# Two of twenty stores cut by partitions: 96 rows in one transfer, 32 rows in four transfers of eight

## The chip, the cores and the metric

The kernel runs on one core of a Trainium2 chip. The metric is the device time of one execution in microseconds (us); less is better. A core has a tensor engine (PE, with its weight loads listed as PEld), a vector engine (DVE), a scalar engine (ACT), GpSimd (POOL) and a sync engine (SP). Transfers between the chip's memory (HBM) and the on-chip buffer (SBUF, 128 partitions) are issued by ACT, SP and POOL and carried out by 16 DMA engines. Products of PE land in PSUM banks and are copied out by DVE or ACT.

## The reference

Inputs are `q`, `k`, `v` of 4 x 6400 x 256 in float32, a temperature `tau` of 1, gate weights (256 x 8), and adapter weights `A` (8 x 256 x 16) and `B` (8 x 16 x 256). The output is 25600 x 256 in float32.

```python
qn = q / (np.linalg.norm(q, axis=1, keepdims=True) + 1e-06)
kn = k / (np.linalg.norm(k, axis=1, keepdims=True) + 1e-06)
s = kn.transpose(0, 2, 1) @ qn / tau            # 256 x 256 for each batch
a = softmax of s over the last axis
x = (v @ a).reshape(25600, 256)

logits = x @ w_gate                             # 8 experts
topk = the two largest of each row;  w = softmax of those two
delta[row] = sum over the two experts e of  w * (x[row] @ A[e]) @ B[e]
return x + delta
```

So each batch needs all of its `q` and `k` before any row of its output can be made: the 256 x 256 matrix `a` is a sum over all 6400 rows. After that, rows of `v` are independent of each other.

## The kernel before

**Tiling.** A batch's 6400 rows lie in SBUF as 128 partitions of 50 chunks: partition p has the 50 consecutive rows from 50 p on. Two chunks are a pair, 25 pairs to a batch, 100 in all. Five pairs are a group: its result tile `ys` is 128 partitions x 10 chunks x 256 floats, so the part of a partition is 10,240 bytes, consecutive in HBM too. There are 20 such groups; the last one is cut into groups of three and two pairs.

**Loads.** POOL issues nearly all loads (lines 148, 149 and 151), and they turn float32 into bf16 on the way. `load_more` issues the next one as soon as its buffer is free: four buffers for slices of `q` and `k`, three for pieces of `v`. SP issues the first chunks of `q` and `k` and the weights.

**Two interleaved streams.** The first batch's Gram matrix (`gram`, line 217) and norms (`square`, `norm`) run alone. Then a loop over slots handles a pair of output work per slot, while the Gram matrices of batches 1, 2 and 3 are worked off beside it, in the slots 0 to 20, 24 to 45 and 49 to 67. For a pair, `transposes` brings `v` onto the other axis (line 366) and copies it to `vT` (line 375 on ACT, 377 on DVE); `logits` and `gating` make the gate of a group; `z_gz`, `gz_t` and `delta` make the adapters' part; `y_mm` (line 488) multiplies by `a`. `delta` adds the adapters' part in the same PSUM bank (line 508), and ACT copies the bank to `ys` (line 512). There are two banks for `y` and two for the transposes.

**Stores.** When a group's last pair has been copied, the group goes onto the list `unsent`. `send` (line 522), called once a slot, issues a store from ACT's queue (line 529) while the list is longer than `keep`. `keep` is 7 until slot 67 and falls by one every four slots after it, so that the stores wait while the loads run, and the first goes out at 145.9 us. The pool of `ys` tiles has nine buffers: the first copy of a group waits until the store of the group nine before it has landed. The last ten pairs are stored in seven smaller transfers from SP's queue (line 516). Store number i of ACT's queue, counted from 0, is group i; its 18 stores are groups 0 to 17.

The order of each engine's instructions is written out by the program. On a queue they are issued in that order, and an instruction that waits on a semaphore holds up all behind it on the same engine. Each transfer raises a semaphore as it lands; the transfers of ACT and SP take eight semaphores in turn.

The change touches `send`, and with it lines 522 to 529.

Of the kernel before, what the change touches and what calls it, by code (L numbers as in the profile page):

```python
# [16 lines left out]
def kernel(  # L17
# [18 lines left out]
    P = 128  # L36
# [11 lines left out]
    GRP = 5  # L48
    QKB, VB, YB = 4, 3, 9
    VP = [18, 16, 16]  # L50
    FIRST = 4
    DEFER = 7

    GRAM = {1: (0, 20), 2: (24, 45), 3: (49, 67)}
    assert B == 4 and NC == 50
# [4 lines left out]
    out_v = out.rearrange("(b p c) d -> b p c d", b=B, p=P)  # L60
# [23 lines left out]
    for b, (first, last) in GRAM.items():  # L84
        n = last - first + 1
# [255 lines left out]
    for b in range(B):  # L341
        f = 0
# [179 lines left out]
    def send(keep):  # L522


        eng = nc.scalar
        while len(unsent) > keep:
            gr = unsent.pop(0)
            c0, n = 2 * (gr["f"] - gr["b"] * NPAIR), 2 * gr["n"]
            eng.dma_start(out_v[gr["b"], :, c0:c0 + n, :], gr["ys"][:, 0:n, :])


    for c in range(0, NC, 2):
# [40 lines left out]
    while nz < NPT or zq is not None or dq is not None:  # L573
# [4 lines left out]
        f, us, fb = (None, 0.0, 0) if behind else at_chain.get(slot, (None, 0.0, 0))  # L578
# [19 lines left out]
        if dq is not None:  # L598
            delta(dq)
        dq, zq = zq, u  # L600
        send(max(0, min(DEFER, DEFER - (slot - GRAM[B - 1][1]) // 4)))
        if behind:
            deal(0.3)
# [52 lines left out]
```

## Time and profile before

| | us |
|---|---|
| Median of three runs | 255.92 (255.84 to 256.08) |
| Profiled execution, timed | 255.87 |
| Its span, first to last instruction | 254.1 |
| Busy: PE / ACT / DVE / POOL | 220.4 / 176.1 / 152.7 / 33.0 |
| ACT's stores: first and last issue | 145.9 / 235.8 |
| ACT's stores: issue to landing, least / median / most | 11.0 / 13.1 / 16.1 |
| SP's last store: issue | 246.12 |
| TensorE's mean granted clock | 0.966 of full speed |

The span is counted from the core's first instruction, and all times of the trace are in us from there. In the page, a row of digits cuts the span into 40 slices and gives the busy share of each in tenths. A line of the stretches' view gives start and end, its length, then for PE, PEld, DVE, ACT and POOL the busy time and the number of instructions, then the granted clock, the mean busy share of the 16 DMA engines, and the GB/s that they moved. A line of the waits' view gives who waited for whom, the sum in us, how many times, and the longest. A row of the queues gives packets, MB, and the time of the packets as a share of 16 engines' span; q0 is POOL's queue, q10 ACT's, q1 SP's, and q8 and q14 carry instructions. The trace also holds every packet's start and duration (without the number of its engine), and every landing: a semaphore of a transfer is raised 16 times.

### The profile page before, as it was taken

The numbers are of one execution on the slowest core, as the hardware profiler recorded it, in microseconds if no ns is written. First come the engines' busy times: TensorE is split into PE (matmuls) and PEld (weight loads), VectorE is DVE, ScalarE is ACT, GpSimd is POOL, SyncE is SP. The second block draws the span as 40 slices with busy tenths as digits, with TensorE's granted clock in tenths as the row PEclk, the third lists the DMA queues.
The fourth block names the chain that finished last, engine by engine and source line by source line (L and its number), as shares of the span: only waits on it lengthen the run. The fifth ranks groups of instructions, "written<-read, shape, count | busy, mean of one in ns | idle before, by whom it ended". The sixth has DMA issues, their size and how long they took to land.

```text
span 254.1 us, 7393 instructions
## 1 busy us (share of the span) xinstructions
PE 220.4 (87%) x3106; PEld 190.2 (75%) x3106; DVE 152.7 (60%) x577; ACT 176.1 (69%) x290; POOL 33.0 (13%) x67
## 2 busy tenths in 40 slices
PE   0787793985999999999999989999999899999950
PEld 0444461775899978989999778989997799998940
DVE  1322235453567678685776876767587876778720
ACT  3434344776488698887878778888867777887860
POOL 8131221112112100110110202000000200000000
PEclk9999998696899999999999999999999999999997
DMA  7999999999999999999999999999999999999995
GB/s 213 223 217 215 212 216 214 213 216 216 210 214 215 223 207 215 218 212 214 215 220 211 214 270 259 236 296 281 255 291 292 389 326 362 414 420 426 423 412 220
DMA packets 13745, 66.80 MB, mean 263 GB/s; under 512 B 2576, under 2 KB 2704, under 8 KB 10384
## 3 DMA queue, kind: packets, MB, share of 16 engines
q0 software_dynamic: 8496, 38.80, 74.8%
q10 hardware_dynamic: 2592, 23.59, 22.4%
q1 hardware_dynamic: 2624, 3.94, 4.7%
q8 instruction: 24, 0.39, 0.6%
q14 instruction: 9, 0.07, 0.1%
HBM read 78.91 MB, written 26.21 MB: 414 GB/s over the span
## 4 chain that ended last, share of the span: by engine, by line
PE 58%; DMA 25%; DVE 7%; ACT 3%; issue 2%; POOL 1%; DVEq 0%; POOLq 0%; ACTq 0%
DMA qk<-in_k_dram 20%; PE y_ps L488 15%; PE acc L217 11%; PE zg L472 7%; PE y_ps L508 7%; PE vT_ps L366 6%; DMA out_dram<-ys 5%; PE zg L496 4%; PE nrm L234 3%; PE vT_ps L387 3%; ACT sq L207 2%; DVE gz L476 2%; ACT ys L512 1%; DVE lm L422 1%; DVE e L418 1%
## 5 line engine op out<-in xcount | busy, mean ns | idle before, releaser
L207 ACT ACTIVATE sq<-qk 128x1024 bf16<-128x1024 bf16 x87 | 89.6, 1054 | 22.1 <-DMA qk<-in_k_dram 16.8
L217 PE MATMUL acc<-qk 128*128 128x256 bf16 x400 | 74.7, 287 | 15.3 <-DMA qk<-in_k_dram 8.8
L512 ACT COPY ys<-y_ps 128x512 f32<-128x512 f32 x100 | 58.8, 588 | 22.9 <-PE y_ps L508 19.7
L488 PE MATMUL y_ps<-a_bf,vT 128*128 128x256 bf16 x400 | 60.3, 273 | 0.3 <-ACT ys L512 0.3
L217 PEld LDWEIGHTS <-qk 128*128 128x128 bf16 x400 | 34.4, 102 | 25.4 <-DMA qk<-in_k_dram 11.8
L476 DVE TENSOR_TENSOR gz<-zg,gate 128x256 bf16<-128x256 f32 x100 | 41.7, 418 | 14.7 <-PE zg L472 13.4
L377 DVE COPY vT<-vT_ps 128x512 bf16<-128x512 bf16 x63 | 26.7, 424 | 28.2 <-PE vT_ps L366 27.6
L234 PEld LDWEIGHTS <-sq 128*128 128x128 bf16 x600 | 36.3, 98 | 7.2 <-ACT sq L207 3.1
L366 PE MATMUL vT_ps<-ident,vt 128*128 128x128 bf16 x400 | 39.5, 223 | 0.9 <-DMA vt<-in_v_dram 0.7
L472 PE MATMUL zg<-wa_sb,vT 128*128 128x128 bf16 x400 | 38.7, 220 | 1.2 <-DVE gzT L502 1.0
L508 PE MATMUL y_ps<-ball_sb,gzT 128*128 128x256 bf16 x200 | 38.2, 273 | 0.0
L234 PE MATMUL nrm<-ones_bf,sq 128*128 128x1 bf16 x600 | 35.9, 165 | 1.2 <-ACT sq L207 1.2
L488 PEld LDWEIGHTS <-vT 128*128 128x128 bf16 x400 | 33.6, 97 | 3.2 <-issue 0.4
L366 PEld LDWEIGHTS <-vt 128*128 128x128 bf16 x400 | 30.2, 99 | 3.4 <-DMA vt<-in_v_dram 0.8
L496 PE MATMUL zg<-ident,gz 128*128 128x128 bf16 x200 | 27.9, 222 | 1.1 <-DVE gz L476 0.6
L375 ACT COPY vT<-vT_ps 128x512 bf16<-128x512 bf16 x37 | 21.7, 587 | 10.3 <-PE vT_ps L366 8.9
L472 PEld LDWEIGHTS <-vT 128*128 128x128 bf16 x400 | 26.1, 97 | 3.4 <-issue 2.2
L502 DVE COPY gzT<-zg 128x256 bf16<-128x256 bf16 x90 | 25.3, 281 | 0.0
L148 POOL DMA_DIRECT2D qk<-in_q_dram x21 | 11.4, 545 | 91.1 <-ACT sq L207 23.6
L209 DVE TENSOR_TENSOR sq<-qk 128x1024 bf16<-128x1024 bf16 x13 | 9.0, 693 | 22.3 <-DMA qk<-in_k_dram 15.4
L496 PEld LDWEIGHTS <-gz 128*128 128x128 bf16 x200 | 15.3, 99 | 2.9 <-DVE gz L476 2.5
L151 POOL DMA_DIRECT2D vt<-in_v_dram x17 | 9.0, 534 | 64.4 <-PE y_ps L508 45.5
(61 smaller groups left out, 183.6 us busy)
## 6 DMA issues: line engine op xcount, KB each, us to landing
out_dram<-ys ACTq DMA_DIRECT2D x18, 1280.0 KB, 13.1
qk<-in_q_dram POOLq DMA_DIRECT2D x18, 640.0 KB, 20.9
qk<-in_k_dram POOLq DMA_DIRECT2D x18, 640.0 KB, 23.1
vt<-in_v_dram POOLq DMA_DIRECT2D x5, 1024.0 KB, 26.9
vt<-in_v_dram POOLq DMA_DIRECT2D x3, 1152.0 KB, 25.3
vt<-in_v_dram POOLq DMA_DIRECT2D x6, 512.0 KB, 22.1
out_dram<-ys SPq DMA_DIRECT2D x3, 512.0 KB, 8.7
out_dram<-ys SPq DMA_DIRECT2D x4, 256.0 KB, 7.6
```

The costliest lines, as they stand in the source:

```text
L207: nc.scalar.activation(sq, src, ACT.Square)
L217: nc.tensor.matmul(acc[b][:, ic, :], t[:, 1, o, ic * P:(ic + 1) * P], t[:, 0, o, :], start=(c == 0 and ic == 0), stop=(c == NC - 1), skip_ ...
L234: nc.tensor.matmul(nrm[b][:, j:j + 1], sq[:, w, c % 2, ic * P:(ic + 1) * P], ones_bf[:, 0:1], start=(c == 0 and j == 0), stop=(c == NC - 1 ...
L366: nc.tensor.matmul(pt[:, ic, sc * P:(sc + 1) * P], vt[:, o + sc, ic * P:(ic + 1) * P], ident, is_transpose=True, start=(i == 0), stop=(i = ...
L377: nc.vector.tensor_copy(dst, src)
L472: nc.tensor.matmul(z[:, sc, :], r["vT"][:, ic, sc, :], st[b]["wa"][:, ic, E:E + ER], start=(sc == 0 and ic == 0), stop=(sc == 1 and ic == ...
L476: nc.vector.tensor_tensor(out=gz.rearrange("p c (e r) -> p c e r", e=E), in0=z.rearrange("p c (e r) -> p c e r", e=E), in1=gr["gate"][:, r ...
L488: nc.tensor.matmul(y[:, sc, :], r["vT"][:, ic, sc, :], st[b]["a"][:, ic, :], start=(sc == 0 and ic == 0), stop=False, skip_group_check=True)
L496: nc.tensor.matmul(gt[:, sc, :], r["gz"][:, sc, :], ident, is_transpose=True, start=(sc == 0), stop=(sc == 1))
L502: nc.vector.tensor_copy(gzT, gt)
L508: nc.tensor.matmul(r["y"][:, sc, :], r["gzT"][:, sc, :], ball_sb, start=False, stop=(sc == 1), skip_group_check=True)
L512: nc.scalar.copy(gr["ys"][:, r["w"]:r["w"] + 2, :], r["y"])
```

## The change

The stores of groups 4 and 9 are issued as five transfers each. The first has partitions 0 to 95; the other four have eight partitions each, 96 to 103 and so on up to 127. All five come from ACT's queue, one after the other, and the bytes are the same. All other stores stay one transfer of 128 partitions.

```diff
     FIRST = 4
     DEFER = 7
+    TILTED = (4, 9)
...
         while len(unsent) > keep:
             gr = unsent.pop(0)
             c0, n = 2 * (gr["f"] - gr["b"] * NPAIR), 2 * gr["n"]
-            eng.dma_start(out_v[gr["b"], :, c0:c0 + n, :], gr["ys"][:, 0:n, :])
+            ends = [0, 96, 104, 112, 120, P] if gr["f"] // GRP in TILTED else [0, P]
+            for p0, p1 in zip(ends, ends[1:]):
+                eng.dma_start(out_v[gr["b"], p0:p1, c0:c0 + n, :], gr["ys"][p0:p1, 0:n, :])
```

`gr["f"]` is the number of a group's first pair among the 100, and `GRP` is 5, so `gr["f"] // GRP` is the group's number.

## The prediction

> **What bounds the kernel now.** I read the page first: engines, DMA rows, queues.
>
> ```profile
> span 254.1 us, 7393 instructions
> PE 220.4 (87%) x3106; PEld 190.2 (75%) x3106; DVE 152.7 (60%) x577; ACT 176.1 (69%) x290; POOL 33.0 (13%) x67
> ...
> DMA  7999999999999999999999999999999999999995
> ...
> q0 software_dynamic: 8496, 38.80, 74.8%
> q10 hardware_dynamic: 2592, 23.59, 22.4%
> q1 hardware_dynamic: 2624, 3.94, 4.7%
> q8 instruction: 24, 0.39, 0.6%
> q14 instruction: 9, 0.07, 0.1%
> HBM read 78.91 MB, written 26.21 MB: 414 GB/s over the span
> ```
>
> No compute engine is full over the span; the 16 DMA engines are, in every slice but the first and last. The queues' shares add up to 103%. So each DMA engine works without a pause from the first load to the last store, and it ends when its own sum of work is done. The page cannot show whether all sixteen end together. Busy time by stretches can; the last two columns are the DMA share and GB/s.
>
> ```profile
> 230.00:245.00 15.00, 14.55 (x187) 12.99 (x185) 10.56 (x49) 12.41 (x31) 0.00 (x0) 1.00 1.00 420
> ...
> 248.00:249.00 1.00, 0.00 (x0) 0.00 (x0) 0.00 (x0) 0.00 (x0) 0.00 (x0) 1.00 1.00 393
> 249.00:249.40 0.40, 0.00 (x0) 0.00 (x0) 0.00 (x0) 0.00 (x0) 0.00 (x0) 1.00 0.86 338
> 249.40:249.80 0.40, 0.00 (x0) 0.00 (x0) 0.00 (x0) 0.00 (x0) 0.00 (x0) 1.00 0.70 282
> ...
> 250.20:250.60 0.40, 0.00 (x0) 0.00 (x0) 0.00 (x0) 0.00 (x0) 0.00 (x0) 0.62 0.61 241
> ...
> 251.40:251.80 0.40, 0.00 (x0) 0.00 (x0) 0.00 (x0) 0.00 (x0) 0.00 (x0) 0.50 0.60 230
> ...
> 252.20:252.60 0.40, 0.00 (x0) 0.00 (x0) 0.00 (x0) 0.00 (x0) 0.00 (x0) 0.50 0.34 128
> 252.60:253.00 0.40, 0.00 (x0) 0.00 (x0) 0.00 (x0) 0.00 (x0) 0.00 (x0) 0.50 0.03 10
> ```
>
> Compute ends before 247. After 249 the DMA share steps down: six engines of sixteen stop by 250.2, ten (0.60 to 0.65) go on to about 252. The last store's semaphore has sixteen landings, one for each engine's share; read from the trace's records, as us after the first at 249.36:
>
> ```
> 0.00 0.06 0.16 0.22 0.28 0.96 | 2.61 2.75 | 3.29 3.32 3.38 3.47 3.55 3.63 3.67 3.69
> ```
>
> Six are early, two in the middle, eight last; the last lands at 253.04, and the timed 255.87 of this execution is 2.83 more (the median of three, 255.92, is 0.05 above it). Where the lags come from: q8 has 24 packets with 0.6% of 16 x 254.1 us, about 1.0 us each. In the records their durations repeat with a period of eight (936, 975, 974, 961, 893, 893, 951, 945 ns, then nearly the same again, twice). I read that as eight engines in turn, three fetches each, some 3.0 us: the last eight. Of the middle two, one ran its 10,240-byte packets at about 420 ns instead of 385 through most of 187 to 246 us; the other, I think, took six of the nine q14 packets, 0.32 us each.
>
> **The change, part by part.** Two stores of 18, the fifth (issued 190.86) and the tenth (208.44), become five transfers each.
>
> Who moves the rows. q10 holds 18 x 128 packets of 10,240 bytes, so a row is a packet and each engine has eight rows of a store today. An eight-row transfer has eight packets and reaches at most eight engines. If all four begin on the same eight, those have 6 + 4 = 10 rows of the group and the others six. Two groups: plus four rows here, minus four there. Nothing in this trace has fewer than 128 rows in a store, so the bounds are: rows spread evenly (0 us), or four more on eight fixed engines, 4 x 0.385 = 1.54 us, with eight more completion packets of 9 to 22 ns (the 4-byte packets of q10), about 0.1: 1.64 us. I take the second, because a transfer of eight equal rows has no reason to begin elsewhere than the last one did. The Trainium skill, page "DMA: Bandwidth & Descriptors", section "Why a DMA increments its semaphore by 16 and not by 1", states that a transfer uses the largest number of engines up to 16 that divides its rows, and on these queues the lowest-numbered ones: 16 for 96 rows, the same eight for eight rows. No run here shows it yet.
>
> What that does to the end. Eight engines get 1.64 us more, but only six are early. At least two of the ten later ones are among the receivers. At best these are the middle two, with the receivers the eight that have no q8 fetches: the later becomes 2.75 + 1.64 = 4.39 after 249.36, against 3.69 now, so +0.70 us; the last eight fall to 3.69 - 1.54 = 2.15, which no longer matters. If one of the last eight is a receiver, the end moves by the whole 1.54 to 1.64. Even work would end near 3.69 - 1.36 = 2.33 (the shares missing from 1.00 between 249.0 and 252.6, in steps of 0.4 us, sum to 3.39 x 0.4 = 1.36 us per engine), but this tilt overshoots: 1.64 is more than the 0.94 between middle and last.
>
> What ACT pays. Issues cost ACT's sequencer this much:
>
> ```profile
> L529 ACTq DMA_DIRECT2D out_dram<-ys x18: 338/338/621, 145.9 to 235.8; - x18
> ...
> DMA to landing us min/median/max: 11.0/13.1/16.1
> ```
>
> The two long ones, 0.57 at 199.33 and 0.62 at 229.13, follow another issue closely. Four more, back to back: 4 x 0.34 = 1.4 to 4 x 0.62 = 2.5 us for each group; I take 2.3, as these follow each other. Behind them queue the copies of line 375 (vT, which frees PE's transpose bank) and line 512 (which frees y). At 190.86 the block is partly covered: ACT sits idle 1.68 us until 194.55 anyway, for the fourth store to land (the only such wait, below). At 208.44 nothing covers it but ACT's slack of about 20%, and PE, busy 9.9 of 10 us from 210, slips by 1 to 2 us. In sum 2 to 3.3 us of compute.
>
> ```profile
> ACT ys L512 <- DMA out_dram<-ys: 1.7, 1, 1.7
> ```
>
> Semaphores. ACT's and SP's transfers take eight semaphores in turn, and one whose predecessor has not landed waits on its queue. Eight more transfers are one whole turn, so the last stores keep their partners. Between, each waits for a nearer one: the thirteenth store (217.76) would need the ninth, landed at 219.23, or 218.4 if two rows fewer lie ahead on the late engines: 0 to 1.5 us on ACT, I take 0.5; PE's transposes and y wait for that. The first copies into the two groups' reused y tiles wait for five landings; their extra waits are 17 ns each.
>
> What hides it: the last SP store is issued at 246.12 and lands 6.9 us later, because the engines have older rows. From an empty queue the first load of the run landed 3.6 us after its issue, with rows twice as long; I take 3.0 for that store. So compute may slip by 3.9 us before it sets the end; 2.5 to 3.8 us fit. If the cover were gone, it would all be added. SP's own stores move with the copies; POOL's queue is issued past 200.0 no more, and its loads of 198.97 to 200.0 come up to two rows (0.8 us) later on receivers, earlier elsewhere.
>
> Against splitting at all speaks the same page, section "Rules for kernel authors": one 128-partition transfer of 1 MiB or more, no splitting by partitions, as both parts run on the same engines. Its section "Anatomy of one DMA — SWDGE (gpsimd) path" has a fixed 2.0 us per transfer for another kind of queue; eight more would be 16 us if they added up. The row here: SP's last two stores, 256 KB each, land 0.63 us apart, 416 GB/s, so a fixed part is not paid one after the other, and in the sum it is nothing.
>
> Sum: 0.70 us on the two middle engines, compute hidden. 255.92 + 0.70 = 256.6.
>
> **Rivals.**
> Receivers include some of the last eight (all, or every second engine). For it: nothing in the trace numbers the engines. Against: two sets of eight would have to cross. 255.92 + 1.54 = 257.5.
>
> No tilt: the small transfers are spread or begin in turn. For it: no 8-row store in the trace. Then only ACT's cost remains, hidden: 255.9 to 256.1.
>
> Faster: the middle two are not late in the run that is timed. The slow packets belong to one engine, come and go (385 ns again between 205 and 218), and the timed runs of before, bound by the last eight, say nothing on them. The end is then the engine at 0.96 + 1.64 = 2.60 after 249.36 against 3.69: 254.8. It decides where both middle lags are under 3.69 - 1.64 = 2.05. Against it: six q14 packets are work that comes in every execution.
>
> ACT's slip beyond its cover: at 5 us of slip, 1.1 over, 257.0. It takes PE to lose more than ACT's whole added issue time.
>
> **How the numbers follow.** Middle engines decide: 0.45 (own range 256.2 to 257.0; a quarter of it within 0.2%). Receivers among the last: 0.20. ACT's slip: 0.03. No tilt: 0.12. Faster: 0.20. A measurement tells about 0.2%, 0.5 us, from no change. Slower: 0.34 + 0.20 + 0.03 + 0.02 of no tilt = 0.59. Same: 0.10 + 0.09 + 0.02 of the faster case = 0.21. Faster: 0.18 + 0.01 + 0.01 = 0.20. The range, 255.1 to 257.7, leaves out most of the faster case (0.14) and the top of the others (0.05).
>
> **What would show it.** Five issues of line 529 at the fifth and tenth store, 0.34 to 0.62 us each. Right: the small transfers' landings come from eight engines only, the lags of the two sets shift by 1.64 + 1.54 = 3.2 us against each other, all engines but two stop by about 251.3, and the DMA share is 0.1 to 0.2 from there to about 253.4. Wrong: a share that falls from 1.00 to nothing within 1 us near 251.5 (faster), ten engines to the end as now (no tilt), or about half of them until 254.6 (receivers late). The prediction fails too if SP's last store goes out after 250.

## The result and the profile after

The changed kernel takes 258.94 us (median; 258.41 to 259.55) against 255.97 for the kernel before: 1.0116 times as long, with a 95% interval of 1.0097 to 1.0136. That is 1.2% slower, 3.0 us. The prediction was 256.6 in a range of 255.1 to 257.7: the sign was right, the added time over four times what was predicted. The profiled execution, the longest of the four, took 259.55 us, 3.68 more than that of before (255.87). Line numbers move by one behind the new constant, by more behind the new loop; the stores of ACT are now issued on line 534, SP's on line 517.

The page of the changed kernel, in this order: span, busy time of the engines, DMA engines in 40 slices, ACT's store queue, and the chain that ended last, by engine. The last line of the fence is the chain of before.

```profile
span 257.8 us, 7405 instructions
...
PE 223.6 (87%) x3106; PEld 192.6 (75%) x3106; DVE 152.7 (59%) x577; ACT 175.9 (68%) x290; POOL 32.6 (13%) x67
...
DMA  7999999999999999999999999999999999999996
...
q10 hardware_dynamic: 2656, 23.59, 22.8%
...
PE 61%; DMA 20%; DVE 7%; ACT 4%; ACTq 3%; issue 3%; POOL 1%; DVEq 0%; POOLq 0%
...
PE 58%; DMA 25%; DVE 7%; ACT 3%; issue 2%; POOL 1%; DVEq 0%; POOLq 0%; ACTq 0%
```

The page looks much like the one before: the same bytes, nearly the same share of each engine, 64 more packets on q10 (the eight new transfers' completions). Only the chain has something new: ACTq, ACT's issuing of transfers, is 3% of it where it was 0%, and DMA is 20% where it was 25%. So the end is no longer set by the transfers alone. Two views say where. The stretches' view of before (first fence) and after (second; columns as in the prediction: PE, PEld, DVE, ACT, POOL, then clock, DMA share, GB/s):

```profile
210.00:220.00 10.00, 9.89 (x143) 9.17 (x141) 7.50 (x33) 8.01 (x17) 0.00 (x0) 1.00 1.05 380
```

```profile
210.00:220.00 10.00, 6.35 (x60) 5.24 (x59) 4.11 (x19) 3.71 (x8) 0.00 (x0) 0.77 1.05 352
220.00:230.00 10.00, 9.90 (x144) 8.99 (x142) 5.66 (x24) 7.34 (x15) 0.00 (x0) 0.89 0.99 386
...
240.00:250.00 10.00, 10.00 (x137) 9.31 (x135) 7.21 (x33) 8.44 (x21) 0.00 (x0) 1.00 0.92 379
250.00:251.00 1.00, 1.00 (x13) 0.83 (x11) 0.73 (x4) 0.95 (x5) 0.00 (x0) 1.00 0.60 244
```

From 210 to 220 us PE does 60 matmuls instead of 143, and its clock is 0.77. From 240 on PE is full and the DMA engines are not: in before they were at 1.00 until 249. Compute has become the bound. What happened at 210 is group 9's store. ACT's timeline of the changed kernel (start, duration, engine and line; the last bracket is the idle time before):

```profile
210.13 0.34 ACTq L534 DMA_DIRECT2D out_dram<-ys  x1
210.39 0.59 ACT L513 COPY ys<-y_ps 128x512 f32<-128x512 f32 x1
210.50 5.01 ACTq L534 DMA_DIRECT2D out_dram<-ys  x4
215.56 0.21 ACT L436 ACTIVATE ed<-dm 128x10 f32<-128x10 f32 x1 [4.58 <-issue]
215.68 0.57 ACT L376 COPY vT<-vT_ps 128x512 bf16<-128x512 bf16 x1
215.68 2.33 ACTq L534 DMA_DIRECT2D out_dram<-ys  x1
```

The 96 rows take the usual 0.34 us to issue, the four small transfers 5.01, and the next group's whole store, 128 rows in one transfer, still 2.33. What stands behind the four in ACT's program waits for them, and ACT is idle for 4.58 us. (Beside the 2.33 us four copies run, so that issue does not hold ACT up as a whole.) First in the queue behind the four is line 436 (435 in before), the exponential of the gating. The chain of waits between 209 and 218 us follows it step by step (start, duration, what):

```profile
by line: ACTq L534 49.3%; PE y_ps L489 14.3%; ACT vT L376 6.3%; ACT ys L513 5.7%; PE zg L497 5.6%; DVE gz L477 3.2%; issue 2.9%; PE vT_ps L367 2.6%; ACT ed L436 2.5%; DVE ed L449 2.4%; PE y_ps L509 2.4%; DVE ed L446 2.1%; PE zg L473 1.2%
...
210.98 0.75 ACTq L534
...
211.76 1.09 ACTq L534
...
212.88 1.20 ACTq L534
...
214.12 1.40 ACTq L534
...
215.56 0.22 ACT ed L436
...
215.80 0.18 DVE ed L446
...
216.23 0.29 DVE gz L477
...
216.56 0.40 PE zg L497 x2
```

DVE waits for ACT's exponential, and PE for DVE's gate. PE's timeline shows the price:

```profile
216.56 0.40 PE L497 MATMUL zg<-ident,gz 128*128 128x128 bf16 x2 [3.55 <-DVE gz L477]
216.78 1.03 PE L489 MATMUL y_ps<-a_bf,vT 128*128 128x256 bf16 x4
...
223.28 0.60 PE L489 MATMUL y_ps<-a_bf,vT 128*128 128x256 bf16 x4
```

PE is idle for 3.55 us, and for some time afterwards four matmuls of line 489 take 1.03 us instead of 0.60, as the granted clock is at half from 215.3 to 222.1. By our estimate the wait and half of the 5.57 us that PE then works at half clock (216.56 to 222.13) make 6.3 us; the delay of the stores grows by 6.46 us from group 9's to group 11's, as the next paragraph lists. The same sum gives 7.4 us in e1_sixteen (5.10 of wait, 4.58 at half clock), 10.5 in e4_stall (7.96 and 5.02) and 4.7 in e7_only9 (3.00 and 3.42), all below, where that delay grows by 7.52, 10.55 and 4.97.

Group 4's store has the same in small: its five issues take 0.34, 0.58, 0.29, 0.72 and 1.95 us, and the next whole store 0.92. Issue times of stores against before show how the delay grows: group 4 +0.86 (there before the first cut store), group 5 +1.28, group 9 +1.69, group 10 +4.54, group 11 +8.15. From there it stays, and SP's last store goes out at 254.21 instead of 246.12, 8.09 later. It lands at 256.75, 2.54 us after its issue, with all sixteen landings within 0.68 us; in before it landed 6.92 us after its issue. So the old queue of rows had covered 6.92 - 2.54 = 4.38 us, and 8.09 - 4.38 = 3.71 us came out at the end (256.75 against 253.04). For this run that is the same subtraction twice; two other kernels below test it. The queue was not quite empty in after: thirteen engines land within 0.18 us, the last three 0.29 to 0.50 us behind them.

A second difference has no place in the prediction. Packets of 10,240 bytes from q10, which take 0.385 to 0.398 us, were counted where they took over 0.6 us, between 210 and 230: 2 of 738 in before, 29 of 663 in after, up to 1.70 us. The count holds for this window alone: from 203 to 206 us after and e4_stall, which cuts no store, have 19 and 17 packets of 0.65 to 0.82 us. Over the whole run it is the longest packet that tells the kernels apart: 0.79 us in before, 1.70 in after. The engines' lag that the prediction spoke of has shrunk to 0.50 us at the end, because there the engines wait for rows.

### The profile page after: what moved, and what is told of

Its sections match the earlier page's. It is cut to its first block, busy times and chain, and to the rows that moved or that the text cites. A ratio compares the mean times of both kernels' runs of the same rounds, so it can differ in the third digit from the quotient of the medians.

```text
span 257.8 us, 7405 instructions
## 1 busy us (share of the span) xinstructions
PE 223.6 (87%) x3106; PEld 192.6 (75%) x3106; DVE 152.7 (59%) x577; ACT 175.9 (68%) x290; POOL 32.6 (13%) x67
## 4 chain that ended last, share of the span: by engine, by line
PE 61%; DMA 20%; DVE 7%; ACT 4%; ACTq 3%; issue 3%; POOL 1%; DVEq 0%; POOLq 0%
PE y_ps L489 16%; PE acc L218 11%; DMA qk<-in_k_dram 11%; DMA vt<-in_v_dram 9%; PE zg L473 8%; PE y_ps L509 7%; PE vT_ps L367 7%; PE zg L497 4%; PE nrm L235 4%; PE vT_ps L388 3%; ACTq L534 3%; DVE gz L477 2%; ACT ys L513 1%; ACT sq L208 1%; ACT vT L376 1%
## 5 line engine op out<-in xcount | busy, mean ns | idle before, releaser
L489 PE MATMUL y_ps<-a_bf,vT 128*128 128x256 bf16 x400 | 61.6, 278 | 1.1 <-ACT ys L513 1.1
L367 PE MATMUL vT_ps<-ident,vt 128*128 128x128 bf16 x400 | 40.1, 225 | 0.9 <-DMA vt<-in_v_dram 0.8
L509 PE MATMUL y_ps<-ball_sb,gzT 128*128 128x256 bf16 x200 | 38.9, 277 | 0.0
L489 PEld LDWEIGHTS <-vT 128*128 128x128 bf16 x400 | 34.3, 99 | 4.3 <-issue 1.2
L367 PEld LDWEIGHTS <-vt 128*128 128x128 bf16 x400 | 30.8, 101 | 3.7 <-DMA vt<-in_v_dram 0.9
L473 PEld LDWEIGHTS <-vT 128*128 128x128 bf16 x400 | 26.6, 98 | 3.5 <-issue 2.2
## 6 DMA issues: line engine op xcount, KB each, us to landing
qk<-in_q_dram POOLq DMA_DIRECT2D x18, 640.0 KB, 20.2
```

Of the source, the lines that this page charges most:

```text
L367: nc.tensor.matmul(pt[:, ic, sc * P:(sc + 1) * P], vt[:, o + sc, ic * P:(ic + 1) * P], ident, is_transpose=True, start=(i == 0), stop=(i = ...
L473: nc.tensor.matmul(z[:, sc, :], r["vT"][:, ic, sc, :], st[b]["wa"][:, ic, E:E + ER], start=(sc == 0 and ic == 0), stop=(sc == 1 and ic == ...
L489: nc.tensor.matmul(y[:, sc, :], r["vT"][:, ic, sc, :], st[b]["a"][:, ic, :], start=(sc == 0 and ic == 0), stop=False, skip_group_check=True)
L509: nc.tensor.matmul(r["y"][:, sc, :], r["gzT"][:, sc, :], ball_sb, start=False, stop=(sc == 1), skip_group_check=True)
```

## The experiments

The theory after this result: **ACT's long issues delay compute beyond its cover**. The rivals: **the tilt** (eight engines with four rows more per cut group), and **the DMA engines**, slower with such transfers whatever ACT does. The first kernels each take one of them out. This table has all kernels, with numbers from the records of one profiled execution each: the sum of the durations of ACT's store issues, when SP's last store was issued, the last landing, the slow packets (10,240 bytes, over 0.6 us, between 210 and 230 us), and the longest packet of 10,240 bytes in the whole run. The ratio is that of the medians to before.

| kernel | ratio, 95% interval | ACT's issues | SP's last issue | last landing | slow packets | longest |
|---|---|---|---|---|---|---|
| before | 1 | 6.6 | 246.12 | 253.04 | 2 | 0.79 |
| after | 1.0116 (1.0097 to 1.0136) | 17.3 | 254.21 | 256.75 | 29 | 1.70 |
| e1_sixteen | 1.0209 (1.0167 to 1.0251) | 19.8 | 257.39 | 259.73 | 38 | 1.62 |
| e2_sp_tilt | 1.0184 (1.0168 to 1.0199) | 6.8 | 249.76 | 257.82 | 34 | 1.43 |
| e3_early | 1.0047 (1.0032 to 1.0062) | 9.3 | 247.55 | 254.51 | 2 | 0.81 |
| e4_stall | 1.0368 (1.0351 to 1.0386) | 6.2 | 258.89 | 261.22 | 1 | 0.81 |
| e5_two | 1.0121 (1.0107 to 1.0135) | 10.6 | 249.53 | 256.83 | 23 | 1.25 |
| e6_only4 | 1.0032 (1.0020 to 1.0043) | 8.9 | 246.02 | 254.09 | 3 | 0.83 |
| e7_only9 | 1.0066 (1.0052 to 1.0080) | 11.7 | 250.83 | 254.41 | 22 | 1.59 |
| e8_five | 1.0030 (1.0020 to 1.0040) | 7.8 | 246.70 | 253.88 | 2 | 0.81 |
| e9_late | 1.0082 (1.0067 to 1.0097) | 10.9 | 250.47 | 255.09 | 21 | 1.50 |
| e10_spaced | 1.0210 (1.0170 to 1.0250) | 20.2 | 250.85 | 258.60 | 35 | 1.88 |
| e11_columns | 1.0021 (1.0010 to 1.0033) | 13.8 | 250.40 | 253.88 | 1 | 0.79 |

All edits are against the changed kernel, but e4_stall's, which is against the kernel before.

### e1_sixteen: the same number of transfers, no tilt

```diff
-            ends = [0, 96, 104, 112, 120, P] if gr["f"] // GRP in TILTED else [0, P]
+            ends = [0, 64, 80, 96, 112, P] if gr["f"] // GRP in TILTED else [0, P]
```

> Groups 4 and 9 are still cut into five transfers on ACT's queue, but at 64, 80, 96 and 112 partitions, so that each can be shared evenly by 16 engines (4 + 1 + 1 + 1 + 1 rows each). If an issue is slow because it uses only eight engines, the five issues of a group take 0.34 + 4 x 0.6 = 2.7 us at most, ACT loses about 2.3 us per group, which SP's late landing hides, and the time is 256.0 to 256.6. If the issues wait for room behind transfers that have not landed, they take about 4 us and 7 us as in the changed kernel, and the time is 258 to 259. If it is the tilt of the rows that costs, the time is 256, whatever the issues take.

261.73 us, slower than after and above the 258 to 259 that was expected for long issues. All five transfers now have a multiple of sixteen rows, and the issues are longer still: 0.48, 1.43, 1.19, 1.69 and 2.02 us for group 9, and 2.46 for the next store. SP's last store is issued 11.27 us later than in before; with the 4.38 us of cover that gives 6.89, and the last landing moved by 6.68. The eight engines are not needed for such a loss, and the subtraction holds to 0.2 us in a kernel that it was not made from.

### e4_stall: the lost time of ACT alone, whole stores

```diff
+    STALL = {4: 13, 9: 28}
...
+    junk = const.tile([P, P], BF16, name="junk")
...
             eng.dma_start(out_v[gr["b"], :, c0:c0 + n, :], gr["ys"][:, 0:n, :])
+            for _ in range(STALL.get(gr["f"] // GRP, 0)):
+                nc.scalar.copy(junk, ident_f)
```

> The kernel before, with both stores whole, and ACT kept busy behind them with copies of a constant into a scratch tile: 13 after the store of group 4 and 28 after that of group 9, at some 0.25 us each about 3.3 and 7 us. The copies are added work, nothing is left out. If ACT's lost time alone makes the change slow, the time is 258 to 259.5 with SP's last store issued near 253. If the tilt and the DMA engines do it, the slip is hidden behind the landing of the last stores and the time stays under 257.

265.26 us, above the expected 258 to 259.5: the copies held ACT for 4.30 and 9.20 us, not 3.3 and 7. From group 4's store to group 5's it is 5.3 us instead of 3.9 (4.3 in after), from group 9's to group 10's 9.8 instead of 2.7 (5.6 in after). SP's last store slipped by 12.77; less 4.38 that is 8.39, and the last landing moved by 8.18. Slow packets: 1. So time that ACT loses here is paid in full beyond the cover, without any cut store. The stretches' view of e4_stall shows the same signs as after, and deeper:

```profile
210.00:220.00 10.00, 3.44 (x44) 2.92 (x42) 2.17 (x11) 8.73 (x29) 0.00 (x0) 0.81 1.05 362
220.00:230.00 10.00, 8.39 (x89) 7.11 (x89) 5.02 (x22) 6.54 (x15) 0.00 (x0) 0.67 0.60 248
```

ACT is busy here with the added copies; PE stands, its clock falls, and then the DMA engines run out of rows (0.60).

### e2_sp_tilt: the small transfers on SP's queue

```diff
-                eng.dma_start(out_v[gr["b"], p0:p1, c0:c0 + n, :], gr["ys"][p0:p1, 0:n, :])
+                q_eng = nc.sync if p0 >= 96 else eng
+                q_eng.dma_start(out_v[gr["b"], p0:p1, c0:c0 + n, :], gr["ys"][p0:p1, 0:n, :])
```

> The same cut as in the change, but the four eight-row transfers go out on SP's queue, which issues nothing between 2.6 us and 238 us; ACT issues the 96 rows alone. If the change lost its time through ACT's queue, ACT's issues fall back to 0.34 us each, compute ends near 246, and what is left is the tilt: eight engines with 1.64 us more, three of them among the late ones by the landings of the changed kernel, so 257.4. If the middle engines were the latest receivers, 256.6. If the cost of the small transfers lies in the DMA engines and not in ACT's queue, 258 to 259 as in the change.

260.82 us. By the theory this kernel should have kept the tilt alone, 257.4, and it is slower than after. SP had nothing to do, so its small transfers went out as soon as their rows were ready, 38 to 77 us ahead of their groups' 96 rows. The stores' lines in the view by source (count, then least, median and longest duration in ns), and then the stretches:

```profile
L535 ACTq DMA_DIRECT2D out_dram<-ys x18: 338/338/771, 144.9 to 238.6; - x18
L535 SPq DMA_DIRECT2D out_dram<-ys x8: 276/308/557, 116.4 to 173.5; - x8
```

```profile
210.00:220.00 10.00, 9.79 (x140) 8.94 (x138) 7.63 (x34) 7.65 (x16) 0.00 (x0) 1.00 1.06 350
...
252.00:254.00 2.00, 0.00 (x0) 0.00 (x0) 0.00 (x0) 0.00 (x0) 0.00 (x0) 0.50 0.46 178
254.00:256.00 2.00, 0.00 (x0) 0.00 (x0) 0.00 (x0) 0.00 (x0) 0.00 (x0) 0.50 0.16 65
```

ACT's issues are short again and PE keeps its pace, 140 matmuls from 210 to 220: that part of the theory holds. But the last copy of results, which ends at 248.90, is 2.8 us later than in before (the delay is there early: group 3's store goes out at 184.40 instead of 181.41), and the last store lands 8.06 us after its issue. At the end a share of 0.46 and then 0.16 of the DMA engines works on. The lags of the sixteen landings of one whole store behind group 9 (issued 213.95) have two outliers:

```
0.00 0.09 0.10 0.16 0.18 0.39 0.99 1.35 1.37 1.78 1.92 2.08 2.34 2.39 | 5.69 6.48
```

The eight small transfers had all landed by 185.47, and the packets over 0.85 us start between 218.6 and 225.7: so it is not small transfers in flight that make packets slow there. What is still cut then is group 9's 96 rows (issued 211.24), among whole stores. So the rival that the DMA engines themselves are slower is true as well. The theory was not wrong for after, but not the whole.

### e3_early: the same cut, at the first two stores

```diff
-    TILTED = (4, 9)
+    TILTED = (0, 1)
```

> The same five transfers from ACT's queue, but for groups 0 and 1, whose stores go out at 145.9 and 160.5 us, each alone on its queue. If an issue on eight engines is slow in itself, the four small ones take 0.7 to 2 us each there too, some 4 us in a row. If they wait behind stores that have not landed, the four take about 0.3 to 0.6 us each, 1.2 to 2.4 in sum, since nothing is ahead of them. The time is then 257.0 to 257.5 from the tilt alone, and 258 or more if ACT's block costs as much as later in the run.

257.32 us. Here no older store is under way when the five transfers go out (group 0 landed at 160.00, group 1 is issued at 161.21), and both effects are gone: slow packets number 2, none takes over 0.81 us, and the issues of the two cut groups take 0.28 to 0.57 us. The view by source has a longest issue of 0.63 us, of a whole store at 230.56 (count, least, median and longest in ns):

```profile
L534 ACTq DMA_DIRECT2D out_dram<-ys x26: 283/338/630, 146.6 to 237.3; - x26
```

What is left is the tilt by itself, as far as the records show. The last landing comes at 254.51, 1.5 us later than in before, and SP's last store waits 6.96 us for it, so compute is still covered. The tilt costs about 1.3 us for two groups (257.32 against 256.06).

### e6_only4 and e7_only9: one cut group each

```diff
-    TILTED = (4, 9)
+    TILTED = (4,)
```

> Only group 4 is cut as in the change. Its issues block ACT for some 3.6 us, of which compute kept 0.8 us in the changed kernel. If compute's slip beyond 4.4 us is what costs, nothing of this shows, and what remains is the tilt of one group: two more rows on three late engines, 0.8 us, so 256.5 to 256.9. If each block costs its own time, or half of the change lies in each group, 257.4 or more.

```diff
-    TILTED = (4, 9)
+    TILTED = (9,)
```

> Only group 9 is cut as in the change. Its issues and the next store's hold ACT for some 7.5 us. In the changed kernel about 6.4 us of compute's slip came from there; less 4.4 us of cover that is 2.0 us, so 257.7 to 258.3. If the tilt alone costs, 256.5 to 256.9 as with group 4.

Group 4 alone costs 0.9 us (256.97 against 256.08), group 9 alone 1.8 (257.88); together 2.7 of the 3.0. Group 4's share is not compute's: SP's last store goes out at 246.02, no later than in before. And e7_only9 met its expected 257.7 to 258.3 only in part by the forecast's reason: SP's last store slips by 4.71, 0.33 beyond the cover, while the last landing moves by 1.37, for the last store lands 3.58 us after its issue. Where the slip is close to the cover, the subtraction gives no more than a lower bound. Group 4's issues in this run are 0.34, 0.58, 0.28, 0.33 and 0.32: the block of 1.95 that after had is not there, though the work ahead of it is the same. Group 9's are long where it is cut alone (ACT's timeline of e7_only9):

```profile
208.63 4.46 ACTq L534 DMA_DIRECT2D out_dram<-ys  x4
213.13 0.21 ACT L436 ACTIVATE ed<-dm 128x10 f32<-128x10 f32 x1 [4.03 <-issue]
```

So group 4's long issues belong to some runs (after, e1_sixteen, e10_spaced), group 9's to every kernel here that cuts it on ACT's queue.

### e5_two: two halves of 64 rows

```diff
-            ends = [0, 96, 104, 112, 120, P] if gr["f"] // GRP in TILTED else [0, P]
+            ends = [0, 64, P] if gr["f"] // GRP in TILTED else [0, P]
```

> Groups 4 and 9 in two transfers of 64 rows each, so one more issue per group and no tilt (16 engines both times). In the run with 64 + 4 x 16 rows the second issue took 0.59 us at group 4 and 1.43 us at group 9. If only the issues' time on ACT matters, compute slips by 1 to 2 us, less than the 4.4 us between the last SP store's 6.9 us to landing and the 2.55 us it takes when nothing is ahead, and the time is 255.9 to 256.4. If a cut store costs by itself in the DMA engines, 256.5 or more.

259.26 us; the expectation of almost nothing is far off. Both halves reach all sixteen engines, four rows each, so there is no tilt. There are two more issues, of 0.60 and 1.46 us. The last copy of results ends on time (at 246.41; 246.09 in before). And yet the last landing is at 256.83, 3.8 us late. Between 210 and 230 there are 23 slow packets, up to 1.25 us. One engine falls behind; its lag in the stores from 208.86 on is 6.66, 7.32, 7.20, 7.12 us, against 3.7 to 3.8 for the last engine in before. It is nearly alone at the end, by the view of stretches:

```profile
252.00:254.00 2.00, 0.00 (x0) 0.00 (x0) 0.00 (x0) 0.00 (x0) 0.00 (x0) 0.50 0.36 139
254.00:256.00 2.00, 0.00 (x0) 0.00 (x0) 0.00 (x0) 0.00 (x0) 0.00 (x0) 0.50 0.09 35
```

A share of 0.09 is 1.4 engines of sixteen. That engine holds up more: SP's last store waits for the landing of the store with which it shares a semaphore (249.47) and goes out at 249.53. This is the clean case of the second cost: compute on time, no tilt, and 1.2% lost in the DMA engines.

### e9_late: after the last load has landed

```diff
-    TILTED = (4, 9)
+    TILTED = (12,)
```

> Only group 12 is cut as in the change; its store goes out near 218 us, when the loads have landed and the stores ahead are some 10 us deep. If the long issues and the slow packets come from a deep queue of stores, the four small issues take 0.8 to 1.5 us each here too and store packets of 0.6 us and more stand behind them: compute slips by 4 to 6 us, and the time is 256.5 to 258. If loads in flight beside it are needed, the issues take 0.3 to 0.6 us, and the time is 256.5 to 256.9 from the tilt.

258.19 us for one cut group, more than group 9 costs and just above the expected 256.5 to 258. Issues: 0.34, then 1.18, 0.68, 0.92 and 0.93. Slow packets: 21. Of the loads 26 small packets are left (0.02 MB from 217 to 222, then none), so neither cost needs them. Four older stores have not landed at 217.86; at group 9's time three in e7_only9 and two in after, at group 4's one, none in e3_early.

### e10_spaced: the small transfers one by one, a slot apart

```diff
+    pieces = []
...
+        if pieces:
+            eng.dma_start(*pieces.pop(0))
...
-            for p0, p1 in zip(ends, ends[1:]):
-                eng.dma_start(out_v[gr["b"], p0:p1, c0:c0 + n, :], gr["ys"][p0:p1, 0:n, :])
+            cut = [(out_v[gr["b"], p0:p1, c0:c0 + n, :], gr["ys"][p0:p1, 0:n, :])
+                   for p0, p1 in zip(ends, ends[1:])]
+            eng.dma_start(*cut[0])
+            pieces.extend(cut[1:])
```

> Groups 4 and 9 are cut as in the change, but of the small transfers ACT issues one per slot, some 1.5 us apart. If the issues are long because they come back to back, each takes 0.34 to 0.6 us now, compute slips by less than 3 us, and the time is that of the tilt, 256.5 to 257.5. If the small transfers clog the queue however they come, issues of 1 us and more remain, in the small ones or in the stores after them, and the time is 258 to 260.

261.39 us, worse than all five at once and above the expected 258 to 260. The issues sum to 20.2 us, and the longest, of 2.70, is a whole store's that follows. ACT's timeline of e10_spaced shows that the issues did not stay apart (line 529 issues the small ones, line 538 the rest):

```profile
211.12 0.30 ACTq L529 DMA_DIRECT2D out_dram<-ys  x1
...
212.33 0.37 ACTq L529 DMA_DIRECT2D out_dram<-ys  x1
...
212.74 1.10 ACTq L538 DMA_DIRECT2D out_dram<-ys  x1
...
213.91 1.20 ACTq L529 DMA_DIRECT2D out_dram<-ys  x1
...
215.19 2.33 ACTq L529 DMA_DIRECT2D out_dram<-ys  x1
...
217.72 2.70 ACTq L538 DMA_DIRECT2D out_dram<-ys  x1
```

The two that begin about 1 us after the one before has ended take 0.30 and 0.37; from the next whole store on each begins within 0.2 us of the end of the one before, and they are long. So this kernel does not rule closeness out, and the records of all kernels here speak for it: of 169 store issues on ACT's queue that begin 2 us or more after the one before has ended, none takes over 0.54 us, and all 37 of 0.9 us or more begin within 0.5 us of it. Closeness is not enough, as e3_early shows. The slow packets (35) come all the same.

### e11_columns: five transfers of all 128 partitions

```diff
-            ends = [0, 96, 104, 112, 120, P] if gr["f"] // GRP in TILTED else [0, P]
-            for p0, p1 in zip(ends, ends[1:]):
-                eng.dma_start(out_v[gr["b"], p0:p1, c0:c0 + n, :], gr["ys"][p0:p1, 0:n, :])
+            ends = [0, 2, 4, 6, 8, n] if gr["f"] // GRP in TILTED else [0, n]
+            for a, z in zip(ends, ends[1:]):
+                eng.dma_start(out_v[gr["b"], :, c0 + a:c0 + z, :], gr["ys"][:, a:z, :])
```

> Groups 4 and 9 go out in five transfers each, but cut by columns: each has all 128 partitions and two of the ten chunks, as SP's last stores have. The rows keep their usual engines and no engine gets more than another; the packets are 2 KB instead of 10 KB. If the number of transfers is what blocks ACT, the issues take about 4 and 7 us per group as with 16 engines, and the time is 258 to 262. If the cut by partitions is what does it, because rows go to other engines than usual, the issues take 0.3 to 0.6 us each, there are no store packets far above their usual time at 216 to 224 us, and the time is 255.9 to 256.5.

256.53 us, 0.2% slower than before, with the issues of one forecast and the time that the other one gave. This kernel separates the two costs. As many transfers, cut the other way, and ACT's issues at group 9 are as long as in after (ACT's timeline):

```profile
209.01 0.34 ACTq L534 DMA_DIRECT2D out_dram<-ys  x1
209.38 4.91 ACTq L534 DMA_DIRECT2D out_dram<-ys  x4
214.46 1.17 ACTq L534 DMA_DIRECT2D out_dram<-ys  x1
```

The stretch from 210 to 220 us shows PE held up nearly as in after (99 matmuls; 60 there), with the clock at 1.00:

```profile
210.00:220.00 10.00, 6.56 (x99) 5.99 (x97) 4.19 (x18) 4.81 (x10) 0.00 (x0) 1.00 1.05 368
```

SP's last store slips by 4.28, just inside the cover of 4.38, and packets stay at 0.385 (one slow one, none over 0.79). So **several transfers in a row** behind older stores make the issues long, whichever way the store is cut; the slow packets come with **the cut by partitions**, where it is made at group 9 or 12 (the kernels that cut groups 0, 1 or 4 alone have none over 0.83 us). PE was held up for 3.44 us and kept its clock, and the delay grows by 3.77 us from group 9's store to group 11's, against 6.46 in after: the wait, without the half clock behind it.

### e8_five: a tilt that should help

```diff
-    TILTED = (4, 9)
+    TILTED = (0,)
...
-            ends = [0, 96, 104, 112, 120, P] if gr["f"] // GRP in TILTED else [0, P]
+            ends = [0, 96, 121, 126, P] if gr["f"] // GRP in TILTED else [0, P]
```

> One early group (0, at 145.9 us, where issues took 0.3 us each) is cut into 96 + 25 + 5 + 2 rows. 25 rows go to five engines, five each. If the small transfers always begin at the same engine, and the five early ones that took eight-row transfers in the changed kernel are the first five, these get 4.4 rows more and all others two rows less: the late engines end 0.77 us earlier and the five at about 2.2 us after the first, so 255.1 to 255.5. If the first five are not the early ones, a late engine gets at least four rows more: 257.3 or above. If only the sixteen-engine part counts and the rest is spread, 255.9 to 256.2.

256.94 us against 256.08, so no gain, and a time that none of the three forecasts had. At the first store, where a cut is cheap, a 25-row transfer should give work to five engines that are early. It did land on five engines (five landings). The last store's landings closed up, but two engines stay 3.65 and 3.85 us late:

```
0 0.10 0.20 | 1.21 to 2.43 (eleven engines) | 3.65 3.85
```

No kernel of this study was faster than before.

## Why the prediction was right in sign and wrong in size

**What bounds the kernel** was right for before: with the stores whole, compute has 4.38 us to spare (3.9 was predicted), and SP's last store lands 2.54 us after its issue in after, 2.33 in e4_stall and 2.34 in e1_sixteen, where the queue is empty but for one to three late engines (3.0 was taken).

**Who moves the rows** was half right. The eight-row transfers do land on eight engines each, as the page "DMA: Bandwidth & Descriptors" of the Trainium skill says in "Why a DMA increments its semaphore by 16 and not by 1". The landings of group 4's first small transfer, as us after its first:

```
0.00 0.05 0.22 0.37 0.56 | 2.25 2.37 2.39
```

But by their lags these are five of the early engines and three of the late ones, not the six early and the two middle ones of the forecast. The rival "receivers include some of the last eight" (257.5, chance 0.20) describes the tilt: e3_early, which has it alone, takes 257.32, and its last landing moves by 1.47 us. The forecast's 0.70 us on the two middle engines was the wrong case, the 1.5 us of the rival the right one. In after neither is what sets the end, so that the sign came out right is in part luck: the step that gave it is not the one that cost the time.

**"What ACT pays" is the step that failed**, and by itself it moves the result out of the range (whether the slow packets would have done so without it is open). It took 2.3 us for four more issues of each group, from two rows of 0.57 and 0.62 where one issue follows another. Measured in after: 3.54 us for group 4's four, 4.91 for group 9's, and 0.58 and 1.99 more than usual for the whole store behind each; 11.0 in all, where the step had 4.6. It then missed what stands in the queue. It named the copies of lines 375 and 512, but the first behind group 9's issues is the exponential of line 435, for which DVE's gate and then PE wait. And PE's long wait was followed by half a clock, for which the step had no term: about 2.8 us, by the estimate above. The step's slip of 2 to 3.3 us was in fact 8.09 - 0.86 = 7.2.

**The cover** was the right test with a wrong input. The rival "ACT's slip beyond its cover" is what happened: its rule, that the excess is paid in full, holds in e4_stall and e1_sixteen. It was given a chance of 0.03, on the argument that PE would have to lose more than ACT's whole added issue time. PE did not: ACT's issue time rose by 10.7 us. The condition was built on the same mis-sized term, so the step and its rival fell together. "SP's last store goes out after 250" was named as the sign of failure, and it went out at 254.21.

**Rows at 0.385 us** was an assumption without a test. The sum counted rows per engine and kept their price. e5_two shows that it changes: no tilt, compute on time, and 3.2 us lost. In after this cost is nearly hidden behind the late compute: the last store lands 2.54 us after its issue, only 0.2 more than in e4_stall and e1_sixteen; in e2_sp_tilt, where the last copy is 2.8 us late and the cover would hide that, it shows.

**Semaphores** cost next to nothing, as predicted at the low end: seven waits of 17 ns on ACT's queue, and no wait of ACT for a landed store from 185 to 250.

**The rule against it.** The Trainium skill's page "DMA: Bandwidth & Descriptors", section "Rules for kernel authors", says not to split by partitions, since both parts use the same engines anyway. That makes a split useless, not harmful. The direction held, and the runs go further: 1.0121 for two halves of 64 partitions, against 1.0021 for five parts by columns.

**What stays open.** What slows the packets, and why most of that falls on one or two engines, is not settled. Nor is what a long issue waits for. It takes another issue close before it, and a count of transfers under way does not fit: e3_early has four or five of its own and no long issue, and group 4's were long in after and short in e6_only4. No kernel here keeps the issues of a cut store 2 us apart, which would be the next test. How after would end with short issues and slow packets was seen only through e2_sp_tilt, where the small transfers also went out far earlier.

## What to carry to other kernels

Leave a store whole; if it must be cut, cut along the free dimension and keep all partitions. Before adding transfers to a queue that still holds older stores, price each issue that follows another closely at 1 to 2 us of the issuing engine (0.7 to 2.7 here), and look up the very next instructions on it and who waits for them. Add what PE loses if its wait brings the clock down. Then compare the slip with the cover, which is the time from the last store's issue to its landing less what that store takes alone.

## What the runs showed of the hardware

An issue of a transfer took 0.28 to 0.57 us for the cut groups of e3_early, with no older store under way. With two to four older stores under way (groups 9 and 12) it took mostly 0.7 to 2.7 us for the second and later ones of a cut group and for a store close behind it. The size did not set it: in after 80 KB took 1.09 to 1.40 us and 1280 KB 2.33, while 1280 KB took 0.34 us where no issue was close before it (243.92).

The granted clock fell to half around PE waits of 2.30 us (e1_sixteen, at 197.49), 2.32 (e2_sp_tilt, at 171.79), 2.64 (e9_late), 3.00 (e7_only9) and 3.55 (after), and it did not fall in e11_columns with one of 3.44; so the length of a wait alone does not decide it. The stretches at half clock lasted 3.41 or 3.42 us in the first four, 6.83 in after and 10.25 in e4_stall. The Trainium skill's page "TensorE: Matmul & The Clock Gate", in "Part 1: The HAM clock gate (the "warmup" mystery)", has about 3.4 us of idleness for the fall and as much sustained work for the return, with a window that is not tied to the kernel. The lengths of the stretches agree with such a window, the falls around waits of 2.3 to 3.0 us do not agree with 3.4 us of idleness; the return in after came 5.6 us after PE's first matmul (216.56 to 222.13).

One late DMA engine reaches back into the issuing queue: in e5_two SP's queue was free at 246.90 and the last copy done at 246.41, and its last store went out at 249.53, after the landing (249.47) of the transfer whose semaphore it takes over.
